# An attention and SwiGLU kernel on one core: the seventh product without its copy, and x's parts for half two at other beats

## The chip, the cores and the metric

The kernel runs on one core of a Trainium2 chip. The metric is the device time of one execution in microseconds (us). A core has a matrix engine (TensorE, PE in the profile; PEld is its weight load), a vector engine (VectorE, DVE), a scalar engine (ScalarE, ACT), GpSimd (POOL), and SyncE (SP), which issues the DMAs here. Each engine runs its instructions in the order of the program and waits for the others through semaphores. TensorE writes into PSUM, which has eight banks; ACT and DVE read and write both PSUM and the on-chip memory SBUF.

## The reference

For one input x of 2048 rows and 576 columns the kernel computes

```python
g = sigmoid((x * gate_w).sum(-1, keepdims=True))
a = infini_attention(x) @ wo          # 32 heads of 18, four segments of 512 rows, softmax inside
                                      # a segment plus a memory of the segments before it
b = (silu(x @ w_gate) * (x @ w_up)) @ w_down      # 576 -> 4608 -> 576
out = g * a + (1 - g) * b
```

All inputs and outputs are float32. The large matmuls are made of three matmuls each, on a high part and a low part of both operands.

## The kernel before

**Stages.** Up to about 207 us the kernel makes q, k and v and the memory of all segments. Then comes the main loop, up to about 1632 us, which runs the SwiGLU part and attention's softmax side by side. At the end the attention output is projected with `wo` and mixed.

**Units.** The main loop has 72 units: two halves of x's rows (`half` 0 and 1, 1024 rows each), and in each half 36 tiles of 128 hidden columns (`f`). They are numbered 0 to 71 here. In a unit the products `x @ w_gate` and `x @ w_up` of one tile, for two blocks of 512 rows, are computed with seven block products instead of eight. Each product is made by `seven`: six matmuls on x's parts and one on the remaining rows. `seven(t, j)` reads part j of x (`XO[j]`, with two column blocks z = 0 and 1, each with a high and a low half) and sums in bank t. The results are combined on ACT and DVE: a bank `a` gets products one, three and five, `xx` starts as a copy of `a` after product one and gets product four, and `y` takes products two and six.

**The seventh product before.** After the fifth product ACT copies bank `a` into the bank of `xx` (L1094), and DVE adds bank `a` to `p5` (L1095). The seventh product adds into `xx`; then DVE multiplies it with the SiLU (L1103). Between the fifth and the seventh product stands the sixth, and in the first unit of three also the down projection of the three tiles before (`down_group`, with its matmuls in L868 and its accumulation on DVE in L878).

**Beats.** Eight times a unit `tick` calls `beat`, which runs the work that was put off to this beat (`defer(k, ...)`: in k beats from now), one step or more of attention (`att_gen`), and down groups. So everything outside the seven products stands in each engine's queue where its beat put it: attention's row maxima (L732, DVE), exponentials (L744, ACT), the halves of the probabilities (L758, DVE and L759, POOL), and the making of the next unit's weights (L264, L268, L271).

**The break.** After unit 35 there are ten beats without a unit (`BREAK`), with down groups and attention. Half two needs seven parts of its own rows of x, in two column blocks. `x_second` loads the raw blocks (`LOADS`), makes sums of them on POOL (`SUMS`, L997), and splits each into a high half on ACT (L136) and a low half on DVE (L137). An entry (o, z, j) of `SUMS` or `PARTS` runs part j of column block z at beat o + 9 counted from the start of unit 34: 10 to 16 is unit 35's last beats and the break, 17 the last beat of the break, 18 to 25 the beats of unit 36, the first of half two. Blocks with z = 0 are in tiles named raw, those with z = 1 in tiles named wo.

Of the kernel before, what the change touches and what calls it, by code (L numbers as in the profile page):

```python
# [16 lines left out]
AF = mybir.ActivationFunctionType  # L17
# [31 lines left out]
SHARE = (0, 0, 2, 2, 3, 3, 3, 3)  # L49
BREAK = 10  # L50
LOADS = ((-3, 0, 0), (-2, 0, 1), (3, 1, 0), (4, 1, 3), (4, 0, 3), (5, 0, 2), (5, 1, 1), (6, 1, 2))
SUMS = ((2, 0, 1), (9, 0, 4), (10, 0, 2), (10, 1, 1), (11, 1, 4), (12, 0, 6), (12, 1, 2), (13, 1, 6))
PARTS = ((1, 0, 0), (4, 0, 1), (10, 1, 0), (10, 0, 5), (11, 0, 3), (11, 1, 5), (12, 1, 3), (13, 0, 4), (14, 0, 2),
         (14, 1, 1), (15, 1, 4), (16, 1, 2), (17, 0, 6), (18, 1, 6))
FIRST = (9, 10, 11, 15, 17, 17, 19)
SLOT = (0, 3, 2, 1, 4, 6, 5)
RPOS = (0, 1, 4, 2, 5, 6, 3)
# [9 lines left out]
def gated_mix(ctx, tc, xT, xrest, wf, wfr, wfh, wd, wv, wo, beta, cmask, ident, bmask, out):  # L67
    nc = tc.nc
# [31 lines left out]
    def banks(*ids):  # L100
        turn = cycle(ids)
        return lambda shape=(P, L): ps.tile(list(shape), F32, name=f"bank{next(turn)}")
# [4 lines left out]
    first_tile = banks(0, 1, 2, 3, 4)  # L107
    lone_tile = banks(7)
    v_tile = banks(5, 6, 7, 4, 0, 5, 6, 7, *8 * (5, 6, 7))
    a_tile = banks(0)  # L110
    x_tile = banks(1)
    y_tile = banks(2)
    taken = {}
    clock = [0]
# [104 lines left out]
    def w_load(f, u):  # L219
        r = raw_tile().rearrange("p (k n) -> p k n", n=P)  # L220
        nc.sync.dma_start(r, wf[f][:, u, 0:4])
        return r
# [30 lines left out]
    def r_fetch(f):  # L253
        nc.sync.dma_start(f32(rhs[f % 2][:96]).rearrange("p j n -> p (j n)"), rc[f // 4, :, f % 4])
# [33 lines left out]
    with ExitStack() as st:  # L288
# [188 lines left out]
        for kt in range(NT):  # L477
            if kt % 2 == 0:
                both = staging(), staging()
            a = both[0][:, L * (kt % 2):L * (kt % 2) + 3 * P].rearrange("p (m n) -> p m n", n=P)  # L480
# [209 lines left out]
    with ExitStack() as st:  # L690
# [15 lines left out]
        def w_fetch(f):  # L706
            ops = wops[1, f] = [None] * 7

            def one(j):
                ops[j] = op_tile()  # L710
                nc.sync.dma_start(f32(ops[j]).rearrange("p a k n -> p (a k n)"), wc[f, j])

            return [(j + 2 if f else FIRST[j], lambda j=j: one(j)) for j in range(7)]
# [268 lines left out]
        def feed(half, f):  # L982
            return [(f // CH, i, hf, hs, ds, yas[half], half) for i in range(8) for hf in range(2)]

        def x_second(new, rest):
            r = {}
            todo = []

            def load(z, q):
                b, kt = ((0, z), (1, z), (0, 2 + z), (1, 2 + z))[q]  # L990
                r[z, q] = wop.tile([P, L], F32, name="wo_") if z else raw_tile()[:, :L]
                nc.sync.dma_start(r[z, q], xT[HALF[1][b], :, kt])

            def total(z, j):
                c, d, e, g = (r.get((z, q)) for q in range(4))
                o, p, q = {1: (c, d, c), 4: (d, g, d), 2: (g, g, c), 6: (e, e, g)}[j]
                nc.gpsimd.tensor_sub(o, p, q)  # L997

            def parts(z, j):
                new[j][z] = x_slot(SLOT[j], z)  # L1000
                split(new[j][z][:, 0], new[j][z][:, 1], r[z, (0, 0, 3, 2, 1, 3, 2)[j]])

            def fetch(j):
                rest[j] = xr_tile(j)
                nc.sync.dma_start(f32(rest[j]), xrd[j])

            todo += [(o, lambda z=z, q=q: load(z, q)) for o, z, q in LOADS]
            todo += [(o, lambda z=z, j=j: parts(z, j)) for o, z, j in PARTS]
            todo += [(o, lambda z=z, j=j: total(z, j)) for o, z, j in SUMS]
            todo += [(6 + j, lambda j=j: fetch(j)) for j in range(7)]  # L1010
            return sorted(todo, key=lambda t: t[0])

        def seven(t, j, first=True):
            w, x = ops[j], XO[j]
            n = 0
            for z in range(2):
                for p, q in ((0, 0), (0, 1), (1, 0)):
                    nc.tensor.matmul(t, w[:, p, z], x[z][:, q], start=first and n == 0, stop=False,  # L1018
                                     skip_group_check=True)
                    n += 1  # L1020
            nc.tensor.matmul(t, rem[:, RPOS[j]], XR[j], start=False, stop=True, skip_group_check=True)  # L1021
# [7 lines left out]
        for pos, (half, f) in enumerate(seq):  # L1029
            if f == 0:  # L1030
                yas[half] = yp.tile([P, 8, D], F32, name="ya")
            q = f % CH
            nxt = seq[pos + 1] if pos + 1 < len(seq) else None
            if q == 0 and f:
                groups += feed(half, f - 1)
                fed.append(f)
            plan = []
            if not nxt:
                plan.append((3, lambda: early.append(c_tr(*tiles.pop(0)))))
            if nxt:  # L1040
                plan += w_fetch(nxt[1]) if nxt[0] and nxt[1] < KEPT else w_make(*nxt)
                if nxt != (0, 1):
                    plan.append((1 if nxt[1] else 10, lambda f=nxt[1]: r_fetch(f)))
                for n, h in enumerate(BLOCKS.get(pos, ())):
                    plan += r_block(h, 4 * n)
                if f + 2 < FT:
                    wraw_of[f + 2] = [None, None]
                    for u in range(2):
                        plan.append(((2, 5)[u] if f or not half else 5 + u, lambda u=u, f=f: wraw_of[f + 2].__setitem__(u, w_load(f + 2, u))))
            if pos == FT - 2:  # L1050
                X2, XR2 = [[None, None] for _ in range(7)], [None] * 7
                plan += [(o + 8, fn) for o, fn in x_second(X2, XR2)]
            for o, fn in plan:
                defer(o + 1, fn)
            step = [0]

            def tick():
                k = step[0]
                step[0] += 1
                if k % 2 == 0 and f and stores:  # L1060
                    nc.sync.dma_start(*stores.pop(0))
                if half == 0:
                    if (q, k) in ((0, 3), (1, 3), (2, 2)):
                        draw[f] = d_load(f)
                    if (q, k) in ((1, 1), (1, 7), (2, 4)):
                        g = f - 1 if k == 1 else f
                        ds[half, g] = d_split(g, draw.pop(g))
                elif (q, k) in ((1, 0), (1, 2), (2, 1)):
                    g = f - 1 if k == 0 else f
                    ds[half, g] = d_fetch(g)  # L1070
                beat(k, half)

            ops, rem = wops.pop((half, f)), rhs[f % 2]
            hh = fp.tile([P, 2, L], F32R, name="hh")
            hl = fp.tile([P, 2, L], F32R, name="hl")
            hs[half, f] = hh, hl
            a, y, xx = a_tile(), y_tile(), x_tile()
            p5, sg0, sg1 = (row_tile() for _ in range(3))
            seven(a, 0)
            nc.scalar.activation(xx, a, AF.Copy)  # L1080
            tick()
            seven(y, 1)
            nc.scalar.activation(p5, y, AF.Copy)
            tick()
            seven(a, 2, False)
            y = y_tile()
            nc.vector.tensor_add(y, a, p5)
            tick()
            seven(xx, 3, False)
            nc.scalar.activation(sg0, xx, AF.Copy)  # L1090
            tick()
            seven(a, 4, False)
            xx = x_tile()
            nc.scalar.activation(xx, a, AF.Copy)  # L1094
            nc.vector.tensor_add(p5, a, p5)  # L1095
            tick()
            nc.scalar.activation(sg0, sg0, AF.Silu)  # L1097
            seven(y, 5, False)
            nc.scalar.activation(sg1, y, AF.Silu)
            tick()  # L1100
            tick()
            seven(xx, 6, False)
            nc.vector.tensor_mul(sg0, xx, sg0)  # L1103
            nc.vector.tensor_mul(sg1, p5, sg1)
            if q == CH - 1:
                defer(2, lambda t=(hh[:, 0], hl[:, 0], sg0): split(*t))
            else:
                split_by(2, hh[:, 0], hl[:, 0], sg0)
            split_by(3, hh[:, 1], hl[:, 1], sg1)
            tick()  # L1110
            assert not groups
            if f == FT - 1:
                groups += feed(half, f)
                if half == 0:
                    for n in range(BREAK):
                        beat(None if n > 1 else n)
                        if n == 0:
                            down_parts([groups.pop(0) for _ in range(3)], CH - 1, CH)
                    XO, XR = X2, XR2
                    assert not groups  # L1120
# [98 lines left out]
```

## Time and profile before

| | |
|---|---|
| median of 3 runs | 1725.83 us (1724.3 to 1725.91) |
| the profiled execution | 1724.43 us, span of the profile 1722.7 us |
| busy: PE, PEld | 1706.5 us, 1481.0 us |
| busy: DVE, ACT, POOL | 1359.8, 1084.8, 938.4 us |
| granted TensorE clock | 1.0 |

A row of the timeline gives start and length in us, engine, line, operation, the tiles (out<-in) and the shape; a bracket tells how long the engine was idle before, and who ended that. A row of the waits gives who waited for whom, the sum in us, how often, and the longest. The end of a matmul is modelled: a matmul of 512 columns is shown with 0.39 us, and the next one starts 0.23 us after it.

### The profile page before, as it was taken

What the parts mean: (1) busy time and instruction counts of PE and PEld (TensorE: products, weight loads), DVE (VectorE), ACT (ScalarE), POOL (GpSimd) and SP (SyncE); (2) the same over time, 40 slices, a digit from 0 to 9 for tenths busy, and PEclk for the clock granted to TensorE, in tenths of its full rate; (3) what the DMA queues carried; (4) which work ended last, traced back from release to release, by engine and by line L of the source; (5) the groups of instructions that cost most, each with busy time, mean ns of one, the idle gap of its engine ahead of it and who ended that gap; (6) DMA issues with size and microseconds to landing.
All of it is one profiled execution on the core that took longest, in us unless ns stands there. A gap on an engine that the chain in (4) does not pass through costs nothing.

```text
span 1722.7 us, 34832 instructions
## 1 busy us (share of the span) xinstructions
PE 1706.5 (99%) x11868; PEld 1481.0 (86%) x11868; DVE 1359.8 (79%) x3231; ACT 1084.8 (63%) x2123; POOL 938.4 (54%) x1194
## 2 busy tenths in 40 slices
PE   9999999999999999999999999999999999999999
PEld 7899978888888888888887888888888888888899
DVE  6557588898899889898989677788887778778655
ACT  7666585776677577667765755765666576566411
POOL 4434646666666656565666555555555555555221
PEclk9999999999999999999999999999999999999999
DMA  8654499999998898988879986887778677767544
GB/s 284 233 186 153 151 311 191 232 226 186 209 227 192 181 215 200 193 198 203 210 144 256 290 177 133 178 186 162 148 181 182 147 157 185 163 132 167 165 144 137
DMA packets 524002, 328.05 MB, mean 190 GB/s; under 512 B 411184, under 2 KB 460336, under 8 KB 523824
## 3 DMA queue, kind: packets, MB, share of 16 engines
q1 hardware_dynamic: 523824, 325.83, 77.5%
q8 instruction: 93, 1.52, 0.4%
q14 instruction: 85, 0.70, 0.1%
HBM read 165.76 MB, written 76.09 MB: 140 GB/s over the span
## 4 chain that ended last, share of the span: by engine, by line
PE 83%; DVE 6%; ACT 5%; DMA 3%; issue 2%; POOL 1%; SPq 1%; DVEq 0%; ACTq 0%; POOLq 0%
PE bank L1018 33%; PE bank L868 24%; PE bank L159 10%; PE bank L1021 5%; PE bank L726 4%; PE bank L774 2%; PE bank L775 1%; PE bank L414 1%; ACT pe L744 1%; ACT L744 1%; PE bank L460 1%; DVE xo L137 1%; DVE p L758 1%; DVE scr L732 1%; PE bank L350 1%
## 5 line engine op out<-in xcount | busy, mean ns | idle before, releaser
L759 POOL TENSOR_TENSOR p<-pe,p 128x512 f16<-128x512 f32 x320 | 376.0, 1175 | 420.4 <-DVE p L758 406.2
L868 PE MATMUL bank<-dw,hh 128*128 128x320 f32 (+1 forms) x2304 | 489.0, 305 | 2.8 <-DVE ya L878 2.8
L868 PEld LDWEIGHTS bank<-dw,hh 128*128 128x128 f32 x2304 | 381.4, 190 | 14.4 <-DVE ya L878 3.8
L744 ACT ACTIVATE pe<-bank,mb 128x512 f32<-128x512 f32 (+3 forms) x512 | 247.9, 526 | 197.7 <-DVE mb L732 191.3
L868 PE MATMUL bank<-dw,hl 128*128 128x320 f32 (+1 forms) x1152 | 340.6, 296 | 0.2 <-DVE hl L137 0.2
L732 DVE CUSTOM_DVE_ANT_0 scr<-bank,cm 128x512 bf16<-128x512 f32 (+3 forms) x512 | 246.6, 482 | 6.8 <-PE bank L726 0.2
L878 DVE TENSOR_TENSOR ya<-bank,ya 128x320 f32<-128x320 f32 x352 | 158.3, 453 | 83.9 <-PE bank L868 83.2
L868 PEld LDWEIGHTS bank<-dw,hl 128*128 128x128 f32 x1152 | 218.0, 189 | 0.4 <-DVE hl L137 0.4
L1021 PE MATMUL bank<-xr,rh 128*128 128x512 f32 x504 | 196.5, 390 | 0.0
L752 POOL TENSOR_SCALAR_AFFINE_SELECT pe<-pe 128x256 f32<-128x256 f32 (+1 forms) x320 | 149.8, 469 | 54.1 <-ACT pe L744 51.0
L758 DVE CAST p<-pe 128x512 f16<-128x512 f32 x320 | 152.5, 477 | 0.0
L264 POOL TENSOR_TENSOR ws<-raw 128x256 f32<-128x256 f32 x140 | 118.3, 845 | 17.4 <-DMA raw<-in_wf_dram 4.5
L726 PE MATMUL bank<-kst,qst 108*128 108x512 bf16 (+3 forms) x512 | 125.2, 306 | 2.1 <-ACT pe L744 2.1
L1021 PEld LDWEIGHTS bank<-xr,rh 128*128 128x128 f32 x504 | 94.7, 188 | 20.3
L963 DVE TENSOR_TENSOR hl<-row,hh 128x512 fp32r<-128x512 f32 x120 | 104.2, 868 | 8.3 <-ACT hh L962 7.8
L1095 DVE TENSOR_TENSOR row<-bank,row 128x512 f32<-128x512 f32 x72 | 49.7, 690 | 64.7 <-ACT bank L1094 64.5
L744 ACT ACT_TABLE_LOAD x69 | 88.5, 1283 | 11.1 <-DVE mb L732 10.1
L1080 ACT ACTIVATE bank<-bank 128x512 f32<-128x512 f32 x72 | 41.9, 582 | 80.5 <-PE bank L1021 77.4
L1090 ACT ACTIVATE row<-bank 128x512 f32<-128x512 f32 x72 | 43.3, 601 | 78.0 <-PE bank L1021 77.8
L1097 ACT ACT_TABLE_LOAD x71 | 91.1, 1283 | 1.3
L264 POOL TENSOR_TENSOR ws<-raw,ws 128x256 f32<-128x256 f32 x70 | 58.3, 833 | 49.4 <-DVE wo__22504 L271 10.9
L159 PE MATMUL bank<-xo,qhi 128*128 128x512 f32 x264 | 83.2, 396 | 0.4 <-ACT vps L399 0.4
(2166 smaller groups left out, 4097.9 us busy)
## 6 DMA issues: line engine op xcount, KB each, us to landing
raw<-in_wf_dram SPq DMA_DIRECT2D x140, 256.0 KB
rh<-rc SPq DMA_DIRECT2D x72, 336.0 KB
dc<-dw SPq DMA_DIRECT2D x36, 576.0 KB
dw<-dc SPq DMA_DIRECT2D x36, 576.0 KB
stk<-q SPq DMA_DIRECT2D x32, 384.0 KB
draw<-in_wd_dram SPq DMA_DIRECT2D x36, 288.0 KB
rc<-rt SPq DMA_DIRECT2D x42, 224.0 KB
vd<-vps SPq DMA_DIRECT2D x8, 912.0 KB
```

Of the source, the lines that this page charges most:

```text
L159: nc.tensor.matmul(t, st[n], mv[n], start=(n == 0), stop=(n == 13))
L264: (nc.gpsimd.tensor_sub if sub else nc.gpsimd.tensor_add)(src[j], p(), q())
L726: nc.tensor.matmul(t[:, c:c + w], qs[:KR, pr, P * i:P * i + P], ks[:KR, pr, 0:w], start=True, stop=True)
L732: nc.vector.tensor_tensor_reduce(scr[:, :w], t[:, c:c + w], cm[:, L - w:L], -SCALE, 3.0e38, OP.add, OP.min, m[:, k:k + 1])
L744: nc.scalar.activation(pe[:, c:c + w], t[:, c:c + w], AF.Exp, bias=m[:, k:k + 1], scale=SCALE)
L752: nc.gpsimd.affine_select(d, d, pattern=pat, compare_op=OP.is_ge, fill=0.0, base=0, channel_multiplier=1)
L758: nc.vector.tensor_copy(p[:, 0], pe)
L759: nc.gpsimd.tensor_sub(p[:, 1], pe, p[:, 0])
L868: nc.tensor.matmul(ts[m], p, q[:, cs], start=(n == 0), stop=(n == 3 * CH - 1))
L878: nc.vector.tensor_add(ya[:, i, cs], t, ya[:, i, cs])
L1018: nc.tensor.matmul(t, w[:, p, z], x[z][:, q], start=first and n == 0, stop=False, skip_group_check=True)
L1021: nc.tensor.matmul(t, rem[:, RPOS[j]], XR[j], start=False, stop=True, skip_group_check=True)
```

## The change

The copy L1094 goes, and the seventh product adds into bank `a` itself. L1095, which reads `a`, must now be done before the seventh product starts. So that the next unit can start while DVE still reads `a`, the two banks change roles from unit to unit (`ax_tile`). For half two, the parts j = 2, 3, 4 and 6 of column block 0 are made later, three of them in unit 36, part 5 of this block three beats later, and most parts of column block 1 one beat sooner; two sums on POOL move with them.

```diff
-SUMS = ((2, 0, 1), (9, 0, 4), (10, 0, 2), (10, 1, 1), (11, 1, 4), (12, 0, 6), (12, 1, 2), (13, 1, 6))
-PARTS = ((1, 0, 0), (4, 0, 1), (10, 1, 0), (10, 0, 5), (11, 0, 3), (11, 1, 5), (12, 1, 3), (13, 0, 4), (14, 0, 2),
-         (14, 1, 1), (15, 1, 4), (16, 1, 2), (17, 0, 6), (18, 1, 6))
+SUMS = ((2, 0, 1), (9, 0, 4), (10, 1, 1), (11, 1, 4), (12, 1, 2), (13, 1, 6), (14, 0, 2), (19, 0, 6))
+PARTS = ((1, 0, 0), (4, 0, 1), (10, 1, 0), (11, 1, 5), (12, 1, 3), (13, 0, 5), (13, 1, 1), (14, 1, 4), (15, 1, 2),
+         (17, 0, 2), (17, 1, 6), (18, 0, 3), (19, 0, 4), (21, 0, 6))
...
-    a_tile = banks(0)
-    x_tile = banks(1)
+    ax_tile = banks(0, 1, 1, 0)
...
-            a, y, xx = a_tile(), y_tile(), x_tile()
+            a, y, xx = ax_tile(), y_tile(), ax_tile()
...
             seven(a, 4, False)
-            xx = x_tile()
-            nc.scalar.activation(xx, a, AF.Copy)
             nc.vector.tensor_add(p5, a, p5)
...
-            seven(xx, 6, False)
-            nc.vector.tensor_mul(sg0, xx, sg0)
+            seven(a, 6, False)
+            nc.vector.tensor_mul(sg0, a, sg0)
```

TensorE in unit 10, from the end of the fifth product (into bank0) over the sixth (bank2) to the seventh and the start of unit 11; first before, then now. `xr` and `rh` belong to the remaining rows, `wo__` to the weights, and the bracket names the engines whose semaphores the instruction waits for.

```order
L1021 MATMUL bank0_5420<-xr4_1616,rh0_2331 128x512
L1018 MATMUL bank2_5531<-xo60_1736,wo__5435 128x512 [waits Activation_49]
L1018 MATMUL bank2_5531<-xo60_1736,wo__5435 128x512
L1018 MATMUL bank2_5531<-xo60_1736,wo__5435 128x512 [waits DVE_49]
L1018 MATMUL bank2_5531<-xo61_1737,wo__5435 128x512 x3
L1021 MATMUL bank2_5531<-xr5_1575,rh0_2331 128x512
L1018 MATMUL bank1_5584<-xo50_2696,wo__5500 128x512 [waits Activation_49]
L1018 MATMUL bank1_5584<-xo50_2696,wo__5500 128x512
L1018 MATMUL bank1_5584<-xo50_2696,wo__5500 128x512 [waits DVE_49]
L1018 MATMUL bank1_5584<-xo51_2717,wo__5500 128x512 x3
L1021 MATMUL bank1_5584<-xr6_1694,rh0_2331 128x512
L1018 MATMUL bank0_5623<-xo00_1110,wo__5537 128x512 [waits DVE_49]
```

```order
L1020 MATMUL bank0_5400<-xr4_1616,rh0_2331 128x512
L1017 MATMUL bank2_5511<-xo60_1736,wo__5415 128x512 [waits Activation_49]
L1017 MATMUL bank2_5511<-xo60_1736,wo__5415 128x512
L1017 MATMUL bank2_5511<-xo60_1736,wo__5415 128x512 [waits DVE_49]
L1017 MATMUL bank2_5511<-xo61_1737,wo__5415 128x512 x3
L1020 MATMUL bank2_5511<-xr5_1575,rh0_2331 128x512
L1017 MATMUL bank0_5400<-xo50_2696,wo__5480 128x512 [waits DVE_49,Activation_49]
L1017 MATMUL bank0_5400<-xo50_2696,wo__5480 128x512 x2
L1017 MATMUL bank0_5400<-xo51_2717,wo__5480 128x512 x3
L1020 MATMUL bank0_5400<-xr6_1694,rh0_2331 128x512
L1017 MATMUL bank1_5601<-xo00_1110,wo__5517 128x512 [waits Activation_49]
```

The matmuls stand in the same order; the seventh product's first one now waits for DVE and writes the bank of the fifth product.

DVE in the same unit, around the addition to `p5` (`row`), before and now:

```order
L732 ISA scr_5573,mb1_2326<-bank4_5568,cm_84 128x384 [waits DVE_49]
L732 ISA mb1_2326 128x1
L1095 TENSOR_TENSOR row_5423<-bank0_5420,row_5423 128x512 [waits Activation_49]
L271 TENSOR_TENSOR wo__5537<-raw_4986,wo__5537 128x256
L271 TENSOR_TENSOR wo__5553<-ws_5505,wo__5553 128x256 [waits Pool_49]
```

```order
L731 ISA scr_5551,mb1_2326<-bank4_5548,cm_84 128x384 [waits DVE_49]
L731 ISA mb1_2326 128x1
L1092 TENSOR_TENSOR row_5403<-bank0_5400,row_5403 128x512 [waits PE_49]
L270 TENSOR_TENSOR wo__5517<-raw_4968,wo__5517 128x256 [waits Activation_49]
L270 TENSOR_TENSOR wo__5533<-ws_5485,wo__5533 128x256 [waits Activation_49]
```

The addition keeps its place behind attention's row maxima; it waits for TensorE's fifth product and no longer for the copy on ACT.

DVE in the break, from its first subtraction for a part of x (`xo`, part slot and column block in the name, so xo60 is part j = 5 of block 0, xo10 is j = 3, xo40 is j = 4), before and now:

```order
L137 TENSOR_TENSOR xo01_13102<-wo__12921,xo01_13102 128x512 [waits DMAHW2_49,Activation_49]
L137 TENSOR_TENSOR xo60_13105<-raw_12937,xo60_13105 128x512 [waits DMAHW5_49,Activation_49]
L963 TENSOR_TENSOR hl_12827<-row_12833,hh_12826 128x512
L878 TENSOR_TENSOR ya_2651<-bank7_13116,ya_2651 128x256 [waits PE_49]
L878 TENSOR_TENSOR ya_2651<-bank4_13127,ya_2651 128x320 [waits PE_49]
L137 TENSOR_TENSOR xo10_13138<-raw_12968,xo10_13138 128x512 [waits DMAHW0_49,Activation_49]
L137 TENSOR_TENSOR xo61_13141<-wo__12935,xo61_13141 128x512 [waits DMAHW4_49,Activation_49]
L878 TENSOR_TENSOR ya_2651<-bank3_13149,ya_2651 128x256 [waits PE_49]
```

```order
L136 TENSOR_TENSOR xo01_13030<-wo__12851,xo01_13030 128x512 [waits DMAHW2_49,Activation_49]
L962 TENSOR_TENSOR hl_12757<-row_12763,hh_12756 128x512
L877 TENSOR_TENSOR ya_2651<-bank7_13040,ya_2651 128x256 [waits PE_49]
L877 TENSOR_TENSOR ya_2651<-bank4_13051,ya_2651 128x320 [waits PE_49]
L136 TENSOR_TENSOR xo61_13062<-wo__12863,xo61_13062 128x512 [waits DMAHW4_49,Activation_49]
L877 TENSOR_TENSOR ya_2651<-bank3_13070,ya_2651 128x256 [waits PE_49]
```

Two subtractions no longer stand ahead of these accumulations `ya`. Further down, xo60 stands ahead of the seventh accumulation from here, and xo10, xo40 and xo50 stand in unit 36.

## The prediction

> **What bounds the kernel now.** I read the page first: the busy shares and the chain that ended last.
>
> ```profile
> span 1722.7 us, 34832 instructions
> PE 1706.5 (99%) x11868; PEld 1481.0 (86%) x11868; DVE 1359.8 (79%) x3231; ACT 1084.8 (63%) x2123; POOL 938.4 (54%) x1194
> PE 83%; DVE 6%; ACT 5%; DMA 3%; issue 2%; POOL 1%; SPq 1%; DVEq 0%; ACTq 0%; POOLq 0%
> ```
>
> TensorE sets the time: it is busy almost without a break, and matmuls are 83% of the chain. An edit on another engine counts only where it shortens or lengthens a wait of PE. So the sum below is one of PE's waits. The two halves of the main loop then show who is close behind (microseconds; PE, PEld, DVE, ACT, POOL busy, granted clock, DMA share):
>
> ```profile
> 230.00:913.00 683.00, 679.03 (x4837) 579.00 (x4835) 599.87 (x1420) 468.49 (x907) 417.63 (x553) 1.00 0.90 205
> 942.00:1632.00 690.00, 687.19 (x4847) 591.18 (x4848) 535.26 (x1316) 434.64 (x841) 368.88 (x472) 1.00 0.75 171
> ```
>
> DVE works 599.87 of 683.00 us in half one (88%) and 535.26 of 690.00 (78%) in half two; ACT has 215 us to spare in half one (683.00 less 468.49). Work that goes over from ACT to the critical order of DVE is dear in half one and cheap in half two. The line that the change takes out, the ACT copy L1094, and who waited for it:
>
> ```profile
> L1094 ACT ACTIVATE bank<-bank x72: 579/582/625, 231.2 to 1629.8; 128x512 f32<-128x512 f32 x72
>   DVE row L1095: 64.5, 57
>   PEld bank L1018: 8.0, 11
>   PE bank L1018: 3.6, 6
> ```
>
> PE itself waited for the copy 3.6 us in 6 places. The other waiter is the DVE addition L1095, 57 times: it reads the same bank as the copy and stands behind it.
>
> **The change part by part: the seventh product.** The copy goes, 72 times 0.58 us of ACT. The seventh product then adds into the bank that L1095 reads, so PE waits for L1095 and for whatever stands ahead of it on DVE. Behind a waiting matmul stands all of PE, down projection and attention included. First a unit where that costs nothing, unit 36 (PE and DVE rows in order of time; the number in brackets is idle time before):
>
> ```profile
> 953.07 0.39 PE L1021 MATMUL bank<-xr,rh 128*128 128x512 f32 x1
> ...
> 954.17 0.69 DVE L1095 TENSOR_TENSOR row<-bank,row 128x512 f32<-128x512 f32 x1 [2.76 <-ACT bank L1094]
> ...
> 956.24 0.39 PE L1021 MATMUL bank<-xr,rh 128*128 128x512 f32 x1
> ```
>
> The fifth product ends at 953.46 and the sixth one's last matmul starts at 956.24, so PE is ready for the seventh at 956.47 (a following matmul starts 0.23 later). DVE stands idle. Without the copy the addition would run from about 953.56 to 954.25, over 2 us early. Now unit 10, in the half where DVE is full:
>
> ```profile
> 423.27 0.59 ACT L1094 ACTIVATE bank<-bank 128x512 f32<-128x512 f32 x1
> ...
> 423.65 0.56 DVE L732 CUSTOM_DVE_ANT_0 scr<-bank,cm 128x384 bf16<-128x384 f32 x1
> ...
> 424.07 0.39 PE L1021 MATMUL bank<-xr,rh 128*128 128x512 f32 x1
> ...
> 424.13 0.69 DVE L1095 TENSOR_TENSOR row<-bank,row 128x512 f32<-128x512 f32 x1
> ...
> 424.30 0.39 PE L1018 MATMUL bank<-xo,wo__5500 128*128 128x512 f32 x1
> ```
>
> The copy ended at 423.86 and PE went on at 424.30 without a wait. L1095 could not start before 424.13, because attention's row maxima (L732) stood ahead of it, and ended at 424.82. With 0.05 to hand over, PE would start at 424.87: 0.57 late. The same working for all 72 units finds 15 late ones; the first is unit 1, the last unit 71:
>
> ```profile
> 243.67 0.39 PE L1021 MATMUL bank<-xr,rh 128*128 128x512 f32 x1
> 244.37 0.69 DVE L1095 TENSOR_TENSOR row<-bank,row 128x512 f32<-128x512 f32 x1
> 244.39 0.50 PE L1018 MATMUL bank<-xo,wo__2816 128*128 128x512 f32 x1 [0.33 <-ACT bank L1094]
> ...
> 1628.65 0.39 PE L1021 MATMUL bank<-xr,rh 128*128 128x512 f32 x1
> 1630.47 0.50 PE L1018 MATMUL bank<-xo,wo__22927 128*128 128x512 f32 x1 [1.43 <-ACT bank L1094]
> ...
> 1630.84 0.69 DVE L1095 TENSOR_TENSOR row<-bank,row 128x512 f32<-128x512 f32 x1
> ```
>
> Unit 1: ready at 243.90, addition done at 245.06, 1.21 late with the hand-over. Unit 71: ready at 1628.88, addition done at 1631.53, 2.70 late. In all (us): units 1: 1.21, 4: 0.42, 10: 0.57, 11: 1.06, 14: 0.51, 17: 0.27, 20: 0.87, 22: 0.26, 23: 0.13, 26: 0.14, 29: 0.59, 31: 0.74, 38: 0.13, 50: 0.50, 71: 2.70, together 10.1. I strike the three under 0.15 (0.4), since DVE no longer waits for copies in the units before (64.5 us in 57 places is 1.1 each): 12 units, 9.7 us. The two waits shown also tell two surcharges. The idle time printed is 0.16 under the lag of the start (244.39 against 243.90, printed 0.33), and the first matmul after a wait lasts 0.50 where others last 0.39, so 0.11 more. After: 9.7 + 12 x 0.11 = 11.0 us. Before: 3.6 + 6 x (0.16 + 0.11) = 5.2 us, all of it gone. Net +5.8 us. The bounds: if ACT's freed time leaves only half of the lateness, 5.5 - 5.2 = +0.3; if one unit more is late for each two that are, 16.5 - 5.2 = +11.3.
>
> On this the Trainium skill, "PSUM — Partial Sum Buffer", section "PSUM bank collisions raise a hardware error", says that two engines may not touch one bank at once, readers included, and that the compiler orders them. The trace agrees: 57 additions stood behind a copy that only reads. Its summary advises another bank for a matmul while one is being read, which speaks against this change.
>
> **The break between the halves.** There PE waits for DVE. The waits of this stretch (919 to 945 us; total, times, longest), then DVE's subtractions for x's parts (L137) and a POOL sum:
>
> ```profile
> PE bank L868 <- DVE ya L878: 2.8, 4, 0.9
> ...
> 926.17 1.33 DVE L137 TENSOR_TENSOR xo<-wo__12921,xo 128x512 fp32r<-128x512 f32 x1
> 927.43 0.89 DVE L137 TENSOR_TENSOR xo<-raw,xo 128x512 fp32r<-128x512 f32 x1
> ...
> 929.57 1.03 DVE L137 TENSOR_TENSOR xo<-raw,xo 128x512 fp32r<-128x512 f32 x1
> 930.02 1.73 POOL L997 TENSOR_TENSOR wo__12921<-wo__12970,wo__12921 128x512 f32<-128x512 f32 x1
> 930.53 1.77 DVE L137 TENSOR_TENSOR xo<-wo__12935,xo 128x512 fp32r<-128x512 f32 x1
> ...
> 936.16 1.05 DVE L137 TENSOR_TENSOR xo<-raw,xo 128x512 fp32r<-128x512 f32 x1
> ...
> 939.59 0.77 DVE L137 TENSOR_TENSOR xo<-raw,xo 128x512 fp32r<-128x512 f32 x1
> ...
> 942.59 0.68 DVE L137 TENSOR_TENSOR xo<-wo__12970,xo 128x512 fp32r<-128x512 f32 x1
> ```
>
> The accumulation L878 frees PE's bank and stands behind these subtractions. The change takes the four with raw (0.89, 1.03, 1.05, 0.77) out of their places and puts one of them back in the middle: 2.85 us less ahead of the last wait. PE's four waits cost 2.8 + 4 x 0.27 = 3.9 us. The first two (under 0.9 each) lose 0.89 and 1.03 of what stands ahead and vanish; of the other two I keep 0.7. Net -3.2 us, between -3.9 and, if DVE only shifts its queue, -1.0.
>
> The parts go to the first unit of half two, where they stand ahead of DVE's L1087, which the fifth product waits for:
>
> ```profile
> 950.38 0.70 DVE L1087 TENSOR_TENSOR bank<-bank,row 128x512 f32<-128x512 f32 x1 [0.39 <-PE bank L1021]
> ...
> 951.71 0.39 PE L1018 MATMUL bank<-xo,wo__13338 128*128 128x512 f32 x1
> ```
>
> L1087 ends at 951.08, 0.63 ahead of the fifth product, and DVE idled 0.39 before it and 2.76 before L1095: about 3 subtractions at 0.68 fit. I take nothing, with up to 0.5 us if that cover is gone. SP's order of DMAs does not change, and no load needs x's staging tiles until that unit's sixth tick, so I take nothing there.
>
> The subtraction of 1.77 us ran beside POOL's sum, the one of 0.68 beside none. The Trainium skill, "SBUF — State Buffer", section "Who interferes with whom", gives a reason: a DVE instruction with two SBUF inputs and a GpSimd one that reads SBUF lock each other out. By that rule each of the two POOL sums moved back frees up to 1.1 us of DVE more, the 0.7 kept would go too, and the sum would be 0.7 lower.
>
> **The sum.** +5.8 - 3.2 = +2.6 us. The profiled execution took 1724.43 us (span 1722.7 and 1.7 around it) and would come to 1727.0. It lies 1.4 under the median of 1725.83 (1724.3 to 1725.91), from which I forecast 1728.4.
>
> **The rivals.**
>
> ```profile
> ACT bank L1080 <- PE bank L1021: 77.4, 51, 13.8
> DVE bank L1087 <- ACT row L1083: 11.4, 12, 1.8
> ```
>
> *DVE late in more units (slower).* Half one has 24 units with only the sixth product as cover; 12 of them are late, by 6.8 us together, 0.56 each. PE's new waits bring work to DVE no sooner, but any DVE order of a few tenths more makes the other 12 late. At half of these, 6 x (0.56 + 0.11) = +4.0 us: +6.6, 1732.4. It decides from two more late units on (+1.3 on the forecast's 2.6 passes 3.45). For it: DVE at 88%. Against: its idle waits for copies go. This is how the rule of the bank would bite.
>
> *ACT's time pays it back (faster).* If additions are late because DVE waited for ACT (12 waits of 11.4 us at L1087), 42 us less on ACT take them away: lateness 4 instead of 11.0, 4 - 5.2 - 3.2 = -4.4, 1721.4. Against: after the copy ACT waits for PE again at L1080 in 51 of 72 units, so its lead is mostly lost within a unit.
>
> *The break gives nothing.* DVE is full there in either order; then +5.8 - 1.0 = +4.8, 1730.6.
>
> **How the numbers follow.** 0.2%, 3.45 us, is about what a measurement of this kernel tells from no change. The forecast has 0.46, its own range 1726 to 1731, a quarter of it over the bound of 1729.3: 0.34 within and 0.12 above. More late units 0.20, the break giving nothing 0.12 (two thirds above), payback 0.22 (0.18 below). So faster 0.18, same 0.42, slower 0.40. The range, 1721.5 to 1734, runs from the payback to a little over the first rival.
>
> **What would show it.** Right: L1095's wait for ACT gone; PE's seventh product waiting for DVE L1095 in some 12 units, mostly of half one, 8 to 11 us; the unit before the end late by 2 to 3 us; PE's waits for L878 in the break under 1 us. Wrong: those PE waits under 5 us or over 16; a wait at the fifth product of the first unit; PE's waits in the break unchanged.

## The result: 0.26% slower, and the profile after

The kernel after takes 1730.42 us in the median of 9 runs (1727.13 to 1732.21), the kernel before 1725.05 in 9 runs beside them (1724.3 to 1725.91). The ratio is 1.0026, 95% interval 1.0018 to 1.0034: slower, by a little more than the 0.2% that a measurement of this kernel can tell (the medians themselves differ by 5.4 us, 0.31%). The forecast was 1728.4, within 1721.5 to 1734.0. The profiled execution of after took 1728.35 us (span 1726.6), 3.9 more than that of before.

The head of the page of after:

```profile
span 1726.6 us, 34785 instructions
PE 1706.3 (99%) x11868; PEld 1480.2 (86%) x11868; DVE 1362.3 (79%) x3231; ACT 1049.1 (61%) x2051; POOL 938.5 (54%) x1194
PE 83%; DVE 6%; ACT 4%; DMA 3%; issue 3%; POOL 1%; SPq 0%; DVEq 0%; POOLq 0%; ACTq 0%
```

ACT's busy time fell by 35.7 us (1084.8 to 1049.1) and PE's is the same: the copies are gone, and the time is longer all the same. The answer is in PE's waits (total, times, longest):

```profile
PE bank L1017 <- DVE row L1092: 7.2, 10, 2.0
PE bank L725 <- ACT pe L743: 2.8, 7, 0.7
PE bank L1017 <- ACT row L1089: 1.0, 1, 1.0
PE bank L1017 <- DVE bank L1086: 0.7, 1, 0.7
...
PE bank L867 <- DVE ya L877: 0.6, 1, 0.6
```

The 3.6 us in 6 places for the copy are gone; 7.2 us in 10 places for the addition L1092 (formerly L1095) are new. L877, the accumulation in the break, went from 2.8 us in 4 places to 0.6 in one. The third row is new and was not forecast; it is unit 36.

The addition itself in the view of its line. It no longer waits for ACT, and where it waits at all, it is for PE's fifth product:

```profile
its engine sat idle before it (us, times) until:
  PE bank L1020: 27.5, 35
who waited for it (us, times):
  PE bank L1017: 7.2, 10
```

Unit 10 again, in the timeline of after. The row maxima (L731) still stood ahead of the addition; PE was ready at 423.31 (0.23 after the start of the sixth product's last matmul), the addition ended at 423.84, and PE started at 423.99, 0.68 late:

```profile
422.67 0.56 DVE L731 CUSTOM_DVE_ANT_0 scr<-bank,cm 128x384 bf16<-128x384 f32 x1
...
423.08 0.39 PE L1020 MATMUL bank<-xr,rh 128*128 128x512 f32 x1
...
423.15 0.69 DVE L1092 TENSOR_TENSOR row<-bank,row 128x512 f32<-128x512 f32 x1
...
423.99 1.40 PE L1017 MATMUL bank<-xo,wo__5480 128*128 128x512 f32 x5 [0.51 <-DVE row L1092]
```

Unit 71, the worst one. Here not the row maxima but a chain through ACT stands ahead: ACT waits for a DMA of `wo`, then makes the halves of another matrix (L135, L169), DVE's L136 and L170 wait for those, and the addition stands behind them:

```profile
1630.70 0.60 ACT L912 ACTIVATE wo<-raw 128x480 fp32r<-128x480 f32 x1 [0.85 <-DMA raw<-in_wo_dram]
...
1631.36 0.39 PE L1020 MATMUL bank<-xr,rh 128*128 128x512 f32 x1
...
1631.82 0.69 DVE L136 TENSOR_TENSOR ol<-bank,oh 128x512 fp32r<-128x512 f32 x1 [2.37 <-ACT oh L135]
...
1632.87 0.69 DVE L1092 TENSOR_TENSOR row<-bank,row 128x512 f32<-128x512 f32 x1
...
1633.70 0.93 PE L1017 MATMUL bank<-xo,wo__22785 128*128 128x512 f32 x3 [1.96 <-DVE row L1092]
```

Unit 36, the first of half two, in the timeline of after: DVE's subtractions for parts 3 and 4, POOL's sum beside the second of them, the fourth product's last matmul, L1086, and the fifth product:

```profile
949.29 0.95 DVE L136 TENSOR_TENSOR xo<-raw,xo 128x512 fp32r<-128x512 f32 x1
...
950.48 1.29 POOL L996 TENSOR_TENSOR raw<-raw 128x512 f32<-128x512 f32 x1
...
950.88 1.45 DVE L136 TENSOR_TENSOR xo<-raw,xo 128x512 fp32r<-128x512 f32 x1 [0.63 <-ACT xo L135]
...
952.76 0.39 PE L1020 MATMUL bank<-xr,rh 128*128 128x512 f32 x1
...
953.39 0.69 DVE L1086 TENSOR_TENSOR bank<-bank,row 128x512 f32<-128x512 f32 x1
...
954.18 0.70 PE L1017 MATMUL bank<-xo,wo__13259 128*128 128x512 f32 x2 [1.03 <-ACT row L1089]
```

PE was ready at 952.99 and started at 954.18. The bracket names ACT's L1089, which began at 953.18 and was done at 953.78; what PE came right after is DVE's L1086, ended at 954.08. L1086 stood behind two subtractions of 0.95 and 1.45 us and 0.63 us of idle time.

In what follows, a product's *lag* is worked out from the starts of all matmuls: how much later its second matmul starts than it would without a wait, lags over 0.06 us summed over the 72 units. The seventh product's lag rose from 6.34 to 12.01 us, the fifth product's from 2.73 to 2.86.

### The profile page after: what moved, and what is told of

It reads as the page before. It is cut to its first block, busy times and chain, and to the rows that moved or that the text cites. A ratio compares the mean times of both kernels' runs of the same rounds, so it can differ in the third digit from the quotient of the medians.

```text
span 1726.6 us, 34785 instructions
## 1 busy us (share of the span) xinstructions
PE 1706.3 (99%) x11868; PEld 1480.2 (86%) x11868; DVE 1362.3 (79%) x3231; ACT 1049.1 (61%) x2051; POOL 938.5 (54%) x1194
## 4 chain that ended last, share of the span: by engine, by line
PE 83%; DVE 6%; ACT 4%; DMA 3%; issue 3%; POOL 1%; SPq 0%; DVEq 0%; POOLq 0%; ACTq 0%
PE bank L1017 32%; PE bank L867 24%; PE bank L158 11%; PE bank L1020 5%; PE bank L725 4%; PE bank L773 2%; PE bank L774 1%; PE bank L459 1%; PE bank L413 1%; ACT L743 1%; DVE hl L962 1%; ACT pe L743 1%; DVE scr L731 1%; POOL p L758 1%; DMA raw<-in_wf_dram 1%
## 5 line engine op out<-in xcount | busy, mean ns | idle before, releaser
L758 POOL TENSOR_TENSOR p<-pe,p 128x512 f16<-128x512 f32 x320 | 375.8, 1174 | 429.1 <-DVE p L757 408.3
L731 DVE CUSTOM_DVE_ANT_0 scr<-bank,cm 128x512 bf16<-128x512 f32 (+3 forms) x512 | 246.0, 481 | 7.1 <-PE bank L725 0.5
L877 DVE TENSOR_TENSOR ya<-bank,ya 128x320 f32<-128x320 f32 x352 | 158.0, 453 | 92.4 <-PE bank L867 91.2
L751 POOL TENSOR_SCALAR_AFFINE_SELECT pe<-pe 128x256 f32<-128x256 f32 (+1 forms) x320 | 152.4, 477 | 51.1 <-ACT pe L743 38.2
L757 DVE CAST p<-pe 128x512 f16<-128x512 f32 x320 | 151.5, 474 | 0.0
L725 PE MATMUL bank<-kst,qst 108*128 108x512 bf16 (+3 forms) x512 | 125.0, 305 | 2.8 <-ACT pe L743 2.8
L1089 ACT ACTIVATE row<-bank 128x512 f32<-128x512 f32 x72 | 43.3, 601 | 79.8 <-PE bank L1020 79.7
L373 POOL TENSOR_TENSOR q<-qr,q 128x512 bf16<-128x512 f32 x36 | 44.4, 1234 | 70.5 <-ACT q L372 58.5
```

Of the source, the lines that this page charges most:

```text
L725: nc.tensor.matmul(t[:, c:c + w], qs[:KR, pr, P * i:P * i + P], ks[:KR, pr, 0:w], start=True, stop=True)
L731: nc.vector.tensor_tensor_reduce(scr[:, :w], t[:, c:c + w], cm[:, L - w:L], -SCALE, 3.0e38, OP.add, OP.min, m[:, k:k + 1])
L751: nc.gpsimd.affine_select(d, d, pattern=pat, compare_op=OP.is_ge, fill=0.0, base=0, channel_multiplier=1)
L757: nc.vector.tensor_copy(p[:, 0], pe)
L758: nc.gpsimd.tensor_sub(p[:, 1], pe, p[:, 0])
L877: nc.vector.tensor_add(ya[:, i, cs], t, ya[:, i, cs])
```

## The experiments

**Each part alone.** First the kernel before with the new tables:

```diff
-SUMS = ((2, 0, 1), (9, 0, 4), (10, 0, 2), (10, 1, 1), (11, 1, 4), (12, 0, 6), (12, 1, 2), (13, 1, 6))
+SUMS = ((2, 0, 1), (9, 0, 4), (10, 1, 1), (11, 1, 4), (12, 1, 2), (13, 1, 6), (14, 0, 2), (19, 0, 6))
...
```

> The kernel before with the two tables of the change (SUMS, PARTS); the copy ahead of the seventh product stays. Theory (the parts of the change add up, each worth what the two traces show at its place): the break gives 3.1 us, the fifth product of unit 36 waits 1.2 us, the seventh products stay at the lag of before (6.3 us in all): 1.9 us faster than before, 1723.1. Rival (DVE is full in the break in either order, and what went there only moved): no gain in the break and the new wait in unit 36, 0 to 1.2 us slower than before.

Measured: 1723.87 us (11 runs, before 1725.43 in 22), ratio 0.9992 (0.9983 to 1.0001), 1.6 us less with an interval that just reaches no change. The waits of its trace show both effects at their places (the copies' wait is L1094 as before):

```profile
PE bank L1018 <- ACT bank L1094: 3.7, 6, 1.4
...
PE bank L1018 <- ACT row L1090: 1.0, 1, 1.0
PE bank L868 <- DVE ya L878: 0.6, 1, 0.6
```

The break's waits are gone as in after, and the new wait in unit 36 is there with the copy too: it belongs to the tables. From the first product of unit 0 to the last seventh product its trace is 0.8 us shorter than that of before (1408.6 against 1409.5 us). Then the kernel after with the tables of before:

```diff
-SUMS = ((2, 0, 1), (9, 0, 4), (10, 1, 1), (11, 1, 4), (12, 1, 2), (13, 1, 6), (14, 0, 2), (19, 0, 6))
+SUMS = ((2, 0, 1), (9, 0, 4), (10, 0, 2), (10, 1, 1), (11, 1, 4), (12, 0, 6), (12, 1, 2), (13, 1, 6))
...
```

> The kernel after with the tables of before: only the copy is gone. Theory (the seventh product waits for whatever stands ahead of L1092's addition on DVE): its lag is 12.0 us against 6.3 before, the break and unit 36 are as before: 5.7 us slower than before, 1730.8. Rival (ACT's freed time pays back, and the loss seen after comes from the tables): 0 to 2 us slower than before. What the median lost beyond the profiled pair (some 1.5 us) should show here too if it belongs to the products, and in the kernel with the tables alone if it belongs to them.

Measured: 1730.85 us (1728.49 to 1732.69), ratio 1.0034 (1.0021 to 1.0046): 5.4 us more. PE's waits:

```profile
PE bank L1017 <- DVE row L1092: 7.8, 10, 2.0
PE bank L867 <- DVE ya L877: 2.8, 4, 1.0
```

The seventh product's lag is 12.40 us, the break's four waits are back, and the fifth product's lag fell to 1.62 us. So the parts add up: the two ratios multiplied are 1.0026, that of after. The copy's removal costs 5.4 us, which is clear of noise; the tables give back 1.6 in the median and 0.8 in the trace, which the times alone do not tell from nothing.

**The copy only where the addition is late.** The kernel after, with the copy in 16 units (`last` is the bank of the seventh product; without a copy the two banks change roles for the next unit):

```diff
+COPIED = (1, 4, 10, 11, 14, 17, 20, 22, 23, 26, 29, 31, 38, 50, 65, 71)
...
             seven(a, 4, False)
+            last = a
+            if pos in COPIED:
+                last = ax[1]()
+                nc.scalar.activation(last, a, AF.Copy)
+            else:
+                ax.reverse()
             nc.vector.tensor_add(p5, a, p5)
```

> The kernel after, with the copy kept in the 16 units where the trace after shows the seventh product later than the copy made it (units 1, 4, 10, 11, 14, 17, 20, 22, 23, 26, 29, 31, 38, 50, 65, 71 of 72), and no copy in the other 56. Theory (late is a unit whose DVE queue holds row maxima or other work ahead of L1092's addition, and only there does the copy earn its keep): in the 16 units the lag is that of before, 4.3 us, in the others near 0.2: 7.5 us faster than after, some 2 to 3 us faster than before. Rival (lateness is a matter of DVE's load and wanders to other units as soon as some are relieved): at least half of the 7.5 stays, so at most 3.7 us faster than after, and seventh products wait in units that are not in the list.

Measured: 1719.59 us (1718.8 to 1722.3), ratio 0.9971 (0.996 to 0.9982): 5.8 us faster than before, where the theory had 2 to 3. The lag of the seventh products is 4.15 us (4.3 to 4.5 expected). It does not wander to other units, but for unit 8 with 0.79; unit 65, with 0.80, is in the list and late in spite of its copy. From the start of unit 0 to the last seventh product the trace is 7.35 us shorter than that of after, where 7.5 was expected. So lateness is tied to the units whose DVE queue holds other work. There the copy frees PE from that queue, since it stands on ACT.

**Unit 36: the part a beat sooner, or later.** First sooner, on the kernel after:

```diff
-         (17, 0, 2), (17, 1, 6), (18, 0, 3), (19, 0, 4), (21, 0, 6))
+         (17, 0, 2), (17, 1, 6), (18, 0, 3), (18, 0, 4), (21, 0, 6))
```

> The kernel after, with part 4 of column block 0 made one beat sooner, in the same beat of unit 36 as part 3 (entry (18, 0, 4) instead of (19, 0, 4)). Theory (L1086 was late in unit 36 because DVE stood 0.63 us idle for the part's high half on ACT, and then ran its subtraction in 1.45 us beside POOL's sum): both subtractions run behind each other, before the sum starts, L1086 ends about 1.2 us sooner and the fifth product of unit 36 no longer waits: 1.2 us faster than after. Rival (DVE's queue there is full with attention's rows whatever the place of the part): the wait stays, and the time with it.

Measured: 1728.70 us (1727.16 to 1731.52, 10 runs), ratio 1.0024 (1.0015 to 1.0033), which is not told apart from after's 1.0026. The fifth product of unit 36 lagged 1.07 us instead of 1.27. The timeline shows why (DVE's two subtractions, the sum, and a DVE cast that reads SBUF):

```profile
950.86 1.76 DVE L136 TENSOR_TENSOR xo<-raw,xo 128x512 fp32r<-128x512 f32 x2
...
952.06 1.72 POOL L996 TENSOR_TENSOR raw<-raw 128x512 f32<-128x512 f32 x1
952.55 1.51 DVE L757 CAST p<-pe 128x512 f16<-128x512 f32 x1
```

The subtractions were shorter and without idle time, as meant; but POOL's sum now fell on the cast, which took 1.51 us where it took 0.41 in after. What DVE won it lost to POOL two instructions on, ahead of the same L1086. The rival was right on the time, the theory on the idle time. Then later, behind L1087, on the kernel with the tables alone:

```diff
-         (17, 0, 2), (17, 1, 6), (18, 0, 3), (19, 0, 4), (21, 0, 6))
+         (17, 0, 2), (17, 1, 6), (18, 0, 3), (20, 0, 4), (21, 0, 6))
```

> The kernel with the tables alone (copy as before), with part 4 of column block 0 made a beat later in unit 36, behind L1087 (entry (20, 0, 4) instead of (19, 0, 4)). Theory (DVE's queue ahead of L1087 is the cause of the wait of 1.26 us there; making the part sooner could not help, since it stayed ahead): 1.45 us of subtraction and 0.63 of idle time leave that place, L1087 is done before the fifth product, which may wait up to 0.3 us for the part itself: 1.0 to 1.3 us faster than the kernel with the tables alone, 1722.7. Rival (the part is now late itself, since ACT makes its high half behind other work): the fifth product waits for ACT or DVE L137 as long as before, no gain.

Measured: 1723.40 us (1722.66 to 1726.22, 11 runs), ratio 0.9993 (0.9984 to 1.0002): no gain against 0.9992. The fifth product's lag in unit 36 fell as expected, from 1.26 to 0.44 us; what is left is its wait for the part itself (0.3 us for DVE's L137 in PE's waits). But the first product of unit 37, without lag before, now lags 0.73. The timeline shows the issue of its weights and its first matmul:

```profile
949.78 0.52 SPq L711 DMA_DIRECT2D wo__13411<-wc  x1
...
955.08 0.47 PE L1018 MATMUL bank<-xo,wo__13411 128*128 128x512 f32 x1 [0.50 <-DMA wo__13411<-wc]
```

PE came sooner and met the load of its weights, which landed some 5.2 us after its issue. In the kernel with the tables alone the same load was issued at 949.21; PE reached this point 6.75 us later, at 955.96, and waited for nothing. The cause of the wait in unit 36 is shown; curing it alone is worth 0.1 us, because a transfer was next in line.

**Both together.** The kernel with chosen copies, unit 8 added, and part 4 a beat later.

> The kernel after with the copy in 17 units (the 16 of the first kernel with chosen copies, and unit 8, which waited 0.79 us there) and part 4 a beat later, as in the kernel above. Theory (the two add up): 1.2 us less in unit 36 and 0.6 less in unit 8: 1.8 us faster than the kernel with 16 copies (1719.6), 1717.8, and 7.5 us faster than before. Rival (what is won in front is lost behind, since DVE's and ACT's queues shift): 1719 to 1720.

Measured: 1721.79 us (1719.92 to 1726.75, 11 runs), ratio 0.9986 (0.9977 to 0.9995): a miss, and on the face of it slower than without the two edits (0.9971). In the trace unit 36 gave 0.83 us and unit 37 took 0.18, but unit 71 lagged 0.95 where it had not lagged, and the loop has the same length as without (1405.8 against 1405.4 us). The two were timed on different chips, so whether the edits lose anything stays open; that they don't gain 1.8 us is shown.

**The beat behind the addition.** No copies at all; in the 16 late units the beat between the fourth and the fifth product is run behind the addition. The work is the same, only the order differs:

```diff
             nc.scalar.activation(sg0, xx, AF.Copy)
-            tick()
+            if pos not in LATE:
+                tick()
             seven(a, 4, False)
             nc.vector.tensor_add(p5, a, p5)
+            if pos in LATE:
+                tick()
             tick()
```

> The kernel after, no copies at all; in the 16 units whose seventh product was late (1, 4, 10, 11, 14, 17, 20, 22, 23, 26, 29, 31, 38, 50, 65, 71) the beat between the fourth and the fifth product is run behind the fifth product and its addition L1092 instead. The work is the same; only what stood ahead of the addition on DVE (attention's row maxima above all) now stands behind it. Theory (the lateness is DVE's order, not its load): the seventh products of these units lose most of their 11.5 us of lag, 2 to 3 us stay; the fifth product loses the cover of the beat and may wait up to 0.2 us more in a unit, 3 us in all: 6 to 9 us faster than after, 1721 to 1724. Rival (DVE is too full in these units, whatever the order): the lag moves to the fifth product or to the next unit, and the time stays within 2 us of after.

Measured: 1718.10 us (1716.61 to 1718.57), ratio 0.9958 (0.9946 to 0.9971), 6.7 us faster than before (1724.80 in 21 runs) and better than the theory's range. The seventh products' lag fell from 12.01 to 0.63 us (all of it in unit 8, which is not in the list), the fifth products' rose by 1.3. Unit 10 in its timeline (the addition is L1094 here), to be held against the one of after above:

```profile
422.04 0.68 DVE L1094 TENSOR_TENSOR row<-bank,row 128x512 f32<-128x512 f32 x1
...
423.27 0.39 PE L1021 MATMUL bank<-xr,rh 128*128 128x512 f32 x1
...
423.40 0.56 DVE L732 CUSTOM_DVE_ANT_0 scr<-bank,cm 128x384 bf16<-128x384 f32 x1
423.50 0.39 PE L1018 MATMUL bank<-xo,wo__5480 128*128 128x512 f32 x1
```

The addition is done at 422.72, 0.78 us before PE is ready, and the row maxima run behind it. The moved beat takes attention's matmuls along, so in 9 of the 16 units PE itself is ready for the seventh product 0.25 to 1.3 us later, counted from the end of the fifth. That alone does not explain the gain: in units 4, 11, 14, 23, 38 and 50 PE is ready as soon as in after, the addition starts 0.3 to 1.3 us sooner, and the lag is gone there too. So the lateness was DVE's order and not its load: DVE is as busy as in after (1366.1 us against 1362.3).

The same in all 72 units:

> The kernel without copies and with the beat behind the fifth product, now in all 72 units instead of the 16 late ones. Theory (the order on DVE is what counts, and it has a price at the fifth product, which loses the beat as cover for L1087): the seventh products have no more lag than with 16 units (0.8 us, unit 8's 0.6 gone too), the fifth products wait up to 0.1 us more in each of the other 56 units, 0 to 5 us in all: 1718 to 1723. Rival (the beat's place costs nothing): 1717 to 1718, the same as with 16 units or a little faster.

Measured: 1717.66 us (1716.36 to 1718.41), ratio 0.9958 (0.9945 to 0.9972). The rival was right: outside the late units the beat's place costs next to nothing (the fifth products' lag is 4.38 us against 4.16, and unit 8's second product lags 0.3), and the list isn't needed. Its second set of runs, on another chip:

> The kernel without copies and with the beat behind the fifth product in all 72 units, unchanged, beside the kernel above for a direct comparison. Theory: 1716.4 to 1718.4 as in its first runs, and the same waits as in its first trace within 0.3 us in each place, since no seventh product stands on the edge. Rival (the spread of these kernels is not tied to the late additions): 1715 to 1720, and waits that differ by more.

Measured: 1718.43 us (1717.41 to 1718.67), ratio 0.9953 (0.9939 to 0.9967). The time is as expected; the waits agree but for unit 5, whose fifth product lagged 0.35 us in one trace and 0.68 in the other. This is the fastest version, beside the one with 16 units: 0.4 to 0.5% faster than before.

**What the copy is worth in this order.** The tables alone (copy in all units), with the beat behind in the 16 units and in 0, 8 and 44, where the copy itself was late:

> The kernel with the tables alone (the copy stays in all units), with the beat behind the fifth product in the 16 late units and in units 0, 8 and 44, where the copy itself was late. It tells what leaving out the copy is worth once the order is right. Theory (copy and addition were both late only for what stood ahead of them on ACT and DVE): the seventh products' 6.3 us of lag fall to about 1, the fifth products gain 1.3 us of waits: some 4 us faster than the kernel with the tables alone, 1719.5 to 1720.5; the copy's removal is then worth 1 to 2 us by itself. Rival (the copy is late because ACT has 42 us more to do): at least 4 us of lag stay, 1722 or more.

Measured: 1722.95 us (1721.7 to 1725.4, 11 runs), ratio 0.9991 (0.9982 to 1.0). Neither theory held whole. The lag of the seventh products is gone, as the first one said; but the time is in the rival's range and no other than that of the tables alone (0.9992). Of the 6.3 us won at the seventh products, the trace shows 1.3 lost at the fifth, 0.7 at the second and 1.2 in front of attention's matmuls. The trace itself is 2.2 us shorter than that of the tables alone from the first product to the last seventh one (1406.4 against 1408.6), but it comes from the fastest of the 11 runs; the rest isn't found. To see this effect alone, the copy in all units and the beat behind in all units:

> The copy stays in all units, and the beat is behind the fifth product in all 72 units: the kernel without copies and with the beat behind everywhere, plus the copy and nothing else. What is leaving out the copy worth in this order? Theory from the traces of the two kernels with the beat behind in 16 and 19 units (3.0 us between the starts of the first product and of the last seventh product): 3 us slower than the kernel without copies, 1720.7. Rival from their medians (1722.95 and 1718.1): 5 us slower, 1722.7. Seventh products have no lag in either case.

Measured: 1732.25 us (1731.37 to 1733.38), ratio 1.0034 (1.0022 to 1.0047), against 1718.43 without the copy on the same chip: the copy costs 13.8 us here, far more than either expectation. The waits of this kernel (L1096 is the copy, L1097 the addition, L1088 the former L1087):

```profile
DVE row L1097 <- ACT bank L1096: 88.9, 67, 2.6
...
PE bank L727 <- ACT pe L745: 4.5, 10, 0.9
...
PE bank L1019 <- DVE bank L1088: 2.9, 7, 0.7
...
PE bank L775 <- ACT pe L745: 1.9, 2, 1.1
```

and of the kernel without the copy (the addition is L1094):

```profile
DVE row L1094 <- PE bank L1021: 50.6, 51, 2.5
...
PE bank L726 <- ACT pe L744: 2.9, 7, 0.7
...
PE bank L1018 <- DVE bank L1087: 1.5, 3, 0.7
```

With the copy DVE stands 88.9 us for the addition, without it 50.6, and a beat's whole DVE work now stands behind this wait. PE pays for it at the fifth product (2.9 against 1.5 us) and in attention (4.5 against 2.9, and 1.9 new): 4.9 us of the 13.8 are in these rows. From the starts of the matmuls, 8 us are in the seven products and 4 in front of attention's matmuls; much of it is in waits too short to have a row. That the copy costs this much in this order is shown; through which waits each part goes is shown for a third of it.

**A second trace of after.**

> The kernel after, unchanged, for a second trace. The three kernels without any copy spread over 4 to 5 us from run to run, those with copies over 2 to 3.5. Theory (some of the new waits stand on the edge: an addition that ends close to the seventh product's time, as in units 8 and 65, which had 0.1 to 0.4 and 0.5 to 1.1 us in three traces): these units differ again, the others agree within 0.1 us, and the time lies between 1727 and 1732. Rival (the spread comes from ahead of the main loop, where the first unit started between 220.9 and 222.7 us): the seventh products agree with the first trace, and the start of unit 0 makes the difference.

Measured: 1728.83 us, span 1727.1. Both theories have a part, and neither foresaw units 4 and 71. The first unit started at 219.88 us (220.95 in the first trace), and the seventh products lagged 12.63 us instead of 12.01: unit 65 0.87 instead of 0.50, unit 71 2.49 instead of 2.19, unit 4 0.38 instead of 0.22, unit 8 none instead of 0.21. The other units agree within 0.03.

## Why the prediction was nearly right

**The seventh product: right, and for the reason given.** Forecast +5.8 us net, measured +5.7 in the trace (12.01 less 6.34), and 5.4 in the median with the products alone. All 12 units counted as late were late, from 0.22 us in unit 4 (0.42 + 0.11 forecast) over 0.75 in unit 10 (0.57 + 0.11) to 2.19 in unit 71 (2.70 + 0.11). That the net fits so closely is in part luck: the sum of after was 1.0 us short (11.0 against 12.01) and that of before 1.1 (5.2 against 6.34, since it counted only the six places that have a row in the waits). In the sum of after two more terms were mis-sized and cancel in part: the hand-over, taken as 0.05 us, is 0.15 in these waits (423.84 to 423.99 in unit 10, 1633.56 to 1633.70 in unit 71), 1.2 us too little in 12 units; and unit 71 was taken 0.6 too late. Two of the struck units came (23 and 38, with 0.28 each; they had been put at 0.13), and units 65 and 8, with 0.50 and 0.21, were not foreseen. The step that carried it, reading from the trace of before where the addition would have ended, was tested directly: with the beat behind the addition the lag is gone in all 16 units.

The Trainium skill, "PSUM — Partial Sum Buffer", section "Summary: rules for kernel authors", advises a different bank for a matmul while one is being read. In the old order the runs agree: dropping the copy costs 5.4 us. As advice on speed it does not hold for every order: with the addition ahead of the beat's work the same bank does no harm, and the copy that avoids it costs 13.8 us.

**The break: right.** Forecast -3.2 us, of which 0.7 was to stay; PE's waits fell from 2.8 us in 4 places to 0.6 in one. With the tables alone 1.6 us remain of it, the difference being unit 36. In the trace of the tables alone the gain over the whole loop is smaller, 0.8 us. The prediction also named 0.7 us more, from two POOL sums that move, after the rule in the Trainium skill, "SBUF — State Buffer", section "Who interferes with whom", on DVE instructions with two SBUF inputs. That did not show: one wait of 0.6 stayed. Only one of the two sums left the break, the other runs later in it, and the wait that stayed stands behind a subtraction beside sums that did not move:

```profile
938.39 1.62 POOL L996 TENSOR_TENSOR wo__12901<-wo__12901,wo__12863 128x512 f32<-128x512 f32 x1
938.78 1.78 DVE L136 TENSOR_TENSOR xo<-wo__12851,xo 128x512 fp32r<-128x512 f32 x1
940.48 0.41 DVE L877 TENSOR_TENSOR ya<-bank,ya 128x256 f32<-128x256 f32 x1
...
940.95 0.56 PE L867 MATMUL bank<-dw,hh 128*128 128x320 f32 x2 [0.57 <-DVE ya L877]
```

**The first unit of half two: wrong.** Forecast 0, up to 0.5; measured 1.27 us. The step that failed was "about 3 subtractions at 0.68 fit". Two errors are in it. Of the idle time that it counted, the 2.76 us lie behind L1087 and could not help it; ahead of L1087 stood 0.39 idle and 0.63 of lead, room for one subtraction of 0.68 more and not for three. And the two subtractions took 0.95 and 1.45 us, the second beside POOL's second moved sum (950.48 to 951.77), while DVE stood 0.63 us for ACT's half between them. The first had ended at 950.24, before the sum began; other work of POOL (L758, L751) ran beside it, and why it took 0.95 was not tested. The price of a sum was in the rows that the prediction itself quoted from the break (0.68 without a sum beside, up to 1.77 with one), and it was not applied to the place to which the sum went.

**What the sum did not hold.** The fifth products of units 5, 8, 29 and 71 lagged 1.1 us less. With the products alone this stays (2.73 to 1.62), so it belongs to the copy: this is all that came of the rival in which ACT's time pays back. Two small waits elsewhere (0.9 in front of L725, 0.5 behind the last unit) go the other way. The traces add up to about +4, the span's 3.9, against +2.6 forecast; unit 36 is most of the difference.

**The medians.** They differ by 5.4 us, the profiled executions by 3.9. Both traces of after come from executions under its median (1728.35 and 1728.83, of runs from 1727.1 to 1732.2), and between these two alone the start of the loop differs by 1.1 us and the seventh products by 0.6. The runs of the two other kernels without any copy in the old order lie 4.2 and 4.4 us apart, those of the tables alone 1.6, those without a copy and with the beat behind 2.1 at most. But two kernels with copies and hardly a late addition scatter by 3.6 and 3.7, and the one with 17 copies and the later part by 6.8, the most of all; so the late additions are not all of it: what makes the slow runs of after stays open.

**The rivals.** Late in more units: units 65, 23 and 38, about 1 us, not the 4 that this rival asked for. The break giving nothing: refuted by the break's waits. Slower was forecast at 0.40 beside 0.42 for no change, and the result, 1.0026, lies just beyond the bound of 0.2% between them.

## What to carry to other kernels

The copy here, a buffer between two engines, was worth what stood ahead of the bank's other reader in that reader's queue. Before such a copy is taken away, list for each place what the reader has queued; then try first to move that work behind the read. With the new tables, the two together won 7 us over the kernel before, and moving the work in all units with the copy kept lost 6; taking the copy away alone lost 5. Neither edit can be judged without the other.

When work is moved to a place with idle time, price it with what will run beside it there, and look for the next thing that would be late: in unit 36 it was POOL's sum, then a load of weights.

## What the runs showed of the hardware

That the slow-down of DVE beside a sum on POOL reaches an instruction with one input: the cast L757 took 0.41 us in unit 36 of after, with no sum beside it, and 1.51 beside a sum of 1.72 in the kernel with the part a beat sooner.

And that PE's hand-over from DVE has more than one price. In all 31 late seventh products of the two traces of after PE starts 0.145 to 0.147 us behind the end of the addition L1092. In the same traces it starts 0.054 or 0.055 us behind the end of L1086 at the late fifth products of units 2, 5, 35 and 62, and in before 0.05 behind the end of the copy in 10 of 11 late seventh products. So the 0.05 of the prediction fits the waits of before, and not the new one. The new seventh product's first matmul waits for two engines, DVE and ACT, the others for one; in the traces its queue has a separate wait for DVE, of 0.05 us, ahead of the weight load. That this makes the difference was not tested.
